# Gated mix of linear and softmax attention on one core: the order of reloads, of the first heads' loads, of the gate and of the linear work

## The chip, the cores and the metric

One core of a Trainium2 chip runs the whole kernel. The metric is the device time of one execution in microseconds (us), the median of several. A core has five engines that run at the same time and meet at semaphores: PE (matrix products), DVE (vector), ACT (scalar functions), POOL (general vector work) and SP (here only a queue that issues DMAs). ACT and POOL issue DMAs as well, each in its own program order.

## The reference

```python
x = A_x                                              # [1, 2048, 1024]
g = _sigmoid((x * gate_w).sum(-1, keepdims=True))    # a gate per row
# A: linear attention, 32 heads of 32, phi(t) = where(t > 0, t + 1, exp(t)) + 1e-6
o_A = (phi(q) @ (phi(k).T @ v)) / (phi(q) @ phi(k).sum(0) + 1e-6)
# B: softmax attention, 32 heads of 32
o_B = softmax(q @ k.T * 32 ** -0.5) @ v
out = g * (o_A @ wo_A) + (1 - g) * (o_B @ wo_B)
```

A and B have their own `wqkv` [1024, 3072] and `wo` [1024, 1024]; all numbers are fp32.

## The kernel before, in words

**Precision.** Each fp32 operand is split into a high and a low part (casts at L304 and L487 on ACT, differences at L299 and L489 on DVE), and a product is three matmuls of 512 columns (`three`, L154, L157, L159). Split operands live in 128x512 places of the large tiles `big0` to `big20`: place 18a is the first half of `big18`, high and low part, 18b the second half.

**Stage A** (to about 563 us) projects x for B and part of A, one half of x's columns at a time (J = 0, then J = 1). For each half there is a pass for v of B with eight weight pieces k = 0 to 7, and then eight "quads" for q and k of B: a quad is seven products (0 to 6) instead of eight. Places for the weights of the quads go round in a ring (`RINGS`): the products 0 to 6 of the last but one quad of the first half use 14a, 19a, 19b, 17b, 14b, 18a, 18b. v's pieces for the second half (`STARTS[1]`) go to 19a, 19b, 17b, 18a, 18b, 14b, 16a, 16b. They were split once and stored in DRAM (`wv0` to `wv7`). `reload_wv` (L822) brings six of them back on ACT's queue (`load_wv_again`, L818), two DMAs each, one piece behind each product from product 1 of that quad on; the last two follow in the last quad.

**Stage B** (from 563 us) is put in order by a planner within the kernel. It keeps a clock for each engine (`T`) and takes steps from four streams: `lin` (linear attention), `max` (row maxima of the scores, matmul L1435 and DVE reduction L1440), `head` (scores again, matmul L1576, then exp on ACT, L1579) and `out` (the projections by `wo`). A head has 64 steps of one `max` and one `head` matmul each; row sums are formed by POOL, whose first sum of a head is L1657 and whose others are L1661; the product with v is L1726. The linear attention's work comes in units of 24 matmuls, in three stages that the text calls kv, q and o (keys, to 1585 us; queries, to 2004 us; output, to 2664 us). After a unit of kv, ACT forms phi (L1315, L1098 to L1100), and DVE (L1321) and POOL (L1326) finish it. How many matmuls of linear attention go with one head step is a number for each stage, `rates`: 2.6 in q (`RATE_Q`), and for kv and o one value that comes out of what is left, (992 + 768 - 24) / (2048 - 320) = 1.005. Nine units of kv are done before the first head step (`WARM_UNITS`), and the maxima start after three of them (`FIRST_UNITS`). Steps that need not be done at once wait in `later` until their planned time (`defer`), or in `tasks`.

**The first heads.** q and k of a head are brought from DRAM (`qk`) to stacks in `big0`/`big1` (head 0) and `big2`/`big3` (head 1): for q 3 pieces for column group 0 and 3 for the rest (`load_q`), for k 3 pieces for each of four column groups (`load_k`), 18 DMAs of together 1.5 MB a head. `load_first` (L1002) issues them on POOL's queue in the steps of `leave`, beside the last quad: the column group 0 of head 0, then that of head 1, each with a step between, then the rest of head 0 and the rest of head 1. Constant rows are set by POOL memsets.

**The gate** is 32 small steps (`gate_step`, L735): SP loads a 128x512 piece of x (`in_xT`), ACT scales it by `gate_w` (L753), POOL adds it up (L759). After every eight, PE sums over the partitions (`total`, L767) and ACT takes the exp (L769). After the last of the four, DVE makes g = 1/(1 + e) and 1 - g (L771 to L773) from it, on 16 columns of SBUF. Gate steps are planned every 2.0 us of planner time from `GATE_FROM` = 4.0 us of stage B on.

Of the kernel before, what the change touches and what calls it, by code (L numbers as in the profile page):

```python
# [12 lines left out]
AF = mybir.ActivationFunctionType  # L13
ALU = mybir.AluOpType
# [6 lines left out]
DH = 32  # L21
# [6 lines left out]

GROUPS, GROUPS_END = (8, 8), (4, 4, 4, 4)
RESERVE = 24.0  # L30
RATE_Q = 2.6
AHEAD = {"head": 0, "max": 6, "lin": 9, "out": 0}
MM = 0.2275
AV, AV_SWITCH = 0.865, 0.35
# [6 lines left out]
NE = 3  # L41
AHEAD_X = 3
PIECE_STEPS, PIECE_REST = (4.0, 3.0), 2
GATE_STEP, GATE_FROM = 2.0, 4.0
LATE = 1.0
MANUAL = {ET.PE, ET.DVE, ET.Activation, ET.SP, ET.Pool}
NMID = 13
# [3 lines left out]
def kernel(  # L51
# [31 lines left out]
    def f32(ap):  # L83
        return ap.bitcast(F32)
# [23 lines left out]
    ones = sb.tile([P, P], F32, name="ones")  # L108
# [5 lines left out]
    g_sb = sb.tile([P, NT], F32, name="g_sb")  # L114
    omg_sb = sb.tile([P, NT], F32, name="omg_sb")
# [12 lines left out]
    bank = [psum.tile([P, C], F32, name=f"bank{i}") for i in range(8)]  # L128
# [34 lines left out]
    def use(eng, cost, *after):  # L163

        T[eng] = max(T[eng], *after, 0.0) + cost
        return T[eng] + LATENCY[eng]

    def dma(to, of):

        T["sp"] = max(T["sp"], T["pe"]) + DMA_ISSUE  # L170
        nc.sync.dma_start(to, of)
# [73 lines left out]
    free = [0.0] * 8  # L245
# [73 lines left out]
    KH = NK // 2  # L319
# [412 lines left out]
    gate_n, gate_at, gate_busy = [0], [GATE_FROM], deque()  # L732
    gate_x, gate_acc = [mid[0], mid[1], mid[8], mid[9], mid[11]], halves(zrep)

    def gate_step():  # L735

        while gate_busy and min(gate_busy)[0] <= T["pe"]:
            first = min(gate_busy)
            gate_busy.remove(first)
            first[-1]()  # L740
        n = gate_n[0]
        if n >= NJ * NK or gate_at[0] > T["pe"]:
            return
        gate_n[0] += 1
        gate_at[0] = T["pe"] + GATE_STEP
        j, k = divmod(n, NK)
        raw, acc = gate_x[n % len(gate_x)], gate_acc[j % 2]
        assert all(at[1] > n - len(gate_x) for at in gate_busy)
        dma(raw, xT[k * P:(k + 1) * P, j * C:(j + 1) * C])

        def times():
            use("act", 0.62, T["pe"])
            nc.scalar.activation(raw if k else acc, raw, AF.Copy, scale=gate_wt[:, k:k + 1])  # L753
            if k:
                plus()

        def plus():
            end = use("pool", 1.3, T["act"] + LATENCY["act"])
            nc.gpsimd.tensor_add(acc, acc, raw)  # L759
            if k == NK - 1:  # L760
                gate_busy.append((end + 0.5, NJ * NK, lambda: tasks.append((bank_at, total))))

        def total():
            b = take()
            end = use("pe", 0.45, free[b])
            for i in range(TPC):
                nc.tensor.matmul(bank[b][:, i:i + 1], acc[:, i * P:(i + 1) * P], ones[:, :1], start=True, stop=True)  # L767
            give(b, use("act", 0.2, end))
            nc.scalar.activation(g_sb[:, j * TPC:(j + 1) * TPC], bank[b][:, :TPC], AF.Exp, scale=-1.0)  # L769
            if j == NJ - 1:  # L770
                nc.vector.tensor_scalar_add(g_sb, g_sb, 1.0)  # L771
                nc.vector.reciprocal(g_sb, g_sb)
                nc.vector.tensor_scalar(omg_sb, g_sb, -1.0, 1.0, op0=ALU.mult, op1=ALU.add)  # L773
                use("dve", 0.4)
                gate_n[0] += 1

        gate_busy.append((T["pe"] + 8.0, n, times))

# [43 lines left out]
    def reload_wv():  # L822

        for _ in range((QUADS - 2) * NP + 1):
            yield
        for k in range(NK - 2):
            load_wv_again(k)
            yield

# [150 lines left out]
    def split_kv(raw, k):  # L980
        split(wpart(k, 0), wpart(k, 1), raw, nc.vector)
# [4 lines left out]
    def leave():  # L986

        split_kv(raw_a[2], 2)
        split_kv(raw_a[3], 3)
        yield  # L990
        split_kv(raw_a[0], 0)
        split_kv(raw_a[1], 1)
        yield
        for k in range(KH, NK):
            split_kv(raw_b[k - KH], k)
            if 0 < k - KH < 3:
                load_first(k - KH - 1, 0)
            yield
        load_first(0, 1)
        load_first(1, 1)  # L1000

    def load_first(h, part):  # L1002

        if not part:
            load_q(h, 0, now=nc.gpsimd)
            load_k(h, 0, nc.gpsimd)
        else:
            load_q(h, 1, NJ, nc.gpsimd)
            for j in range(1, NJ):
                load_k(h, j, nc.gpsimd)  # L1010

    T["sp"] = 0.0

# [366 lines left out]
    tasks = []  # L1380
# [5 lines left out]
    def load_q(h, j, j1=0, now=None):  # L1386

        g, r = divmod(h, 4)
        j1 = max(j + 1, j1)
        q, sl = q_cols(h, j, j1), slice(j * C, j1 * C)  # L1390
        if h < (2 if j else 3):
            nc.gpsimd.memset(f32(q[3 * DH:, :]), 0.0)
        else:
            dma(f32(q[3 * DH:3 * DH + 2, :]), f32(q[3 * DH + 2:3 * DH + 4, :]))
        for b, p in enumerate((0, 0, 1)):
            (now.dma_start if now else dma)(f32(q[b * DH:(b + 1) * DH, :]), qk_d[0][p][g][r * DH:(r + 1) * DH, sl])
        for i in range(j, j1):
            q_ready[h][i] = max(T["pe"] + 8.0, T["sp"] + 5.0)

    def load_k(h, j, now=None):  # L1400

        g, r = divmod(h, 4)
        k = k_stack[h % 2]
        if h < 2 and j == 0:
            nc.gpsimd.memset(f32(k[3 * DH:, :]), 0.0)
            nc.gpsimd.memset(f32(k[3 * DH:3 * DH + 2, :]), 1.0)
        sl = slice(j * C, (j + 1) * C)
        for b, p in enumerate((0, 1, 0)):
            (now.dma_start if now else dma)(f32(k[b * DH:(b + 1) * DH, sl]), qk_d[1][p][g][r * DH:(r + 1) * DH, sl])
        k_ready[h][j] = max(T["pe"] + 6.0, T["sp"] + 4.0)  # L1410

    def v_tile(h):
# [515 lines left out]
    def output():  # L1928
# [55 lines left out]
        for i, (name, n) in enumerate(seq):  # L1984
# [4 lines left out]
            if name == "X21" and n:  # L1989
                load_ra(n + 1)  # L1990

    quad(1, QUADS - 1, beside(leave(), parts))
    assert next(parts, None) is None
    xh_t[2] = sb.tile([P, 2 * HK * P], F32R, name="xh")
    T["sp"] = 0.0
# [2 lines left out]
    for h in range(2):  # L1998
# [121 lines left out]
```

## Time and profile before

| | |
|---|---|
| three runs | 2836.68, 2837.31, 2838.13 us; median 2837.31 us |
| profiled execution | 2837.45 us, of which the span of the trace is 2835.7 us; granted PE clock 0.996 |
| stage kv, 643 to 1585 us | PE busy 933.69 of 942.00 us, POOL 906.13, DVE 796.48, ACT 644.17 |
| stage q, 1585 to 2004 us | PE busy 418.04 of 419.00 us, POOL 373.02 |
| stage o, 2004 to 2664 us | PE busy 659.61 of 660.00 us, POOL 598.99 |

A row of the timeline gives start and length in us, engine, line of the kernel, operation and, in brackets, how long the engine had been idle and on whom it waited. A matmul's recorded length includes the time in the pipeline: at full clock, matmuls of 512 columns stand some 0.23 us apart and read 0.39 us long. A row of the waits gives the waiting line, what it waited for, the total in us, the number of times and the longest. A row of the windows gives the length of the stretch, then busy time and count of PE, its weight loads, DVE, ACT and POOL, the granted clock, the DMA engines' mean busy share and GB/s. A row of the groups gives busy time, mean length in ns and the idle time ahead.

### The profile page before, as it was taken

What the parts mean: (1) busy time and instruction counts of PE and PEld (TensorE: products, weight loads), DVE (VectorE), ACT (ScalarE), POOL (GpSimd) and SP (SyncE); (2) the same over time, 40 slices, a digit from 0 to 9 for tenths busy, and PEclk for the clock granted to TensorE, in tenths of its full rate; (3) what the DMA queues carried; (4) which work ended last, traced back from release to release, by engine and by line L of the source; (5) the groups of instructions that cost most, each with busy time, mean ns of one, the idle gap of its engine ahead of it and who ended that gap; (6) DMA issues with size and microseconds to landing.
All of it is one profiled execution on the core that took longest, in us unless ns stands there. A gap on an engine that the chain in (4) does not pass through costs nothing.

```text
span 2835.7 us, 46700 instructions
## 1 busy us (share of the span) xinstructions
PE 2801.9 (99%) x15784; PEld 2013.6 (71%) x15784; DVE 2267.4 (80%) x3715; ACT 1664.9 (59%) x3167; POOL 2109.6 (74%) x1151
## 2 busy tenths in 40 slices
PE   9998999989999999999999999999999999999999
PEld 8887888876666666676666777676666666676687
DVE  6696759768888888888888877787888888787678
ACT  4333433336676666776666666666767667676622
POOL 0162017468999999999999988998999999999000
PEclk9999999999999999999999999999999999999999
DMA  8587658682443333433334445566544445333774
GB/s 268 174 270 258 202 158 270 222 231 90 103 107 85 86 89 96 114 96 85 85 96 114 142 141 170 172 197 196 168 124 128 128 132 144 101 101 112 261 236 149
DMA packets 391051, 432.77 MB, mean 153 GB/s; under 512 B 105550, under 2 KB 237902, under 8 KB 389020
## 3 DMA queue, kind: packets, MB, share of 16 engines
q1 hardware_dynamic: 366252, 387.69, 45.7%
q0 software_dynamic: 22256, 37.89, 6.2%
q10 hardware_dynamic: 2304, 4.20, 0.4%
q8 instruction: 126, 2.06, 0.3%
q14 instruction: 113, 0.93, 0.1%
HBM read 287.31 MB, written 127.93 MB: 146 GB/s over the span
## 4 chain that ended last, share of the span: by engine, by line
PE 91%; DVE 4%; DMA 3%; ACT 1%; POOL 1%; issue 1%; SPq 0%; ACTq 0%; POOLq 0%; DVEq 0%
PE bank L1726 16%; PE bank L1576 16%; PE bank L1435 15%; PE bank L154 12%; PE bank L157 12%; PE bank L159 12%; PE bank L644 5%; DVE mx L1440 2%; DMA big<-qk 1%; PE bank L1499 1%; ACT big L1579 1%; PE bank L1229 1%; DMA big<-ra 0%; PE bank L1118 0%; DMA big<-big 0%
## 5 line engine op out<-in xcount | busy, mean ns | idle before, releaser
L1661 POOL TENSOR_TENSOR big<-big,big 128x512 f32<-128x512 f32 (+2 forms) x694 | 1641.9, 2370 | 65.4 <-ACT big L1579 19.9
L1440 DVE TENSOR_REDUCE mx<-bank 128x1 f32<-128x512 f32 x2048 | 1285.1, 685 | 282.8 <-PE bank L1435 280.2
L1579 ACT ACTIVATE big<-bank 128x512 f32<-128x512 f32 x2048 | 1156.5, 602 | 349.4 <-PE bank L1576 289.0
L1435 PE MATMUL bank<-big,big 128*128 128x512 f32 x1888 | 743.7, 396 | 13.3 <-DMA big<-qk 7.9
L1576 PE MATMUL bank<-big,big 128*128 128x512 f32 x1888 | 736.2, 396 | 1.0 <-ACT big L1579 0.3
L154 PE MATMUL bank<-big,big 128*128 128x512 f32 x1408 | 552.5, 392 | 10.5 <-DMA big<-wv 8.0
L157 PE MATMUL bank<-big,big 128*128 128x512 f32 x1408 | 551.0, 391 | 0.0
L159 PE MATMUL bank<-big,big 128*128 128x512 f32 x1404 | 549.3, 391 | 1.1 <-DVE big L299 1.1
L1726 PE MATMUL bank<-big,mid 128*32 128x512 f32 x4096 | 454.5, 593 | 0.0
L1576 PEld LDWEIGHTS bank<-big,big 128*128 128x128 f32 x1888 | 353.8, 188 | 125.6 <-issue 45.3
L1435 PEld LDWEIGHTS bank<-big,big 128*128 128x128 f32 x1888 | 355.6, 188 | 101.8 <-DVE mx L1440 12.9
L1726 PEld LDWEIGHTS bank<-big,mid 128*32 128x32 f32 x4096 | 133.4, 110 | 277.4 <-issue 276.0
L154 PEld LDWEIGHTS bank<-big,big 128*128 128x128 f32 x1408 | 265.3, 188 | 71.9 <-DMA big<-wv 8.4
L159 PEld LDWEIGHTS bank<-big,big 128*128 128x128 f32 x1404 | 264.7, 189 | 58.4 <-DVE big L299 2.4
L157 PEld LDWEIGHTS bank<-big,big 128*128 128x128 f32 x1408 | 265.4, 188 | 56.1 <-issue 0.8
L1677 DVE TENSOR_TENSOR bank<-bank,big 128x512 f32<-128x512 f32 x364 | 253.1, 695 | 6.4 <-ACT big L1579 1.4
L304 ACT CAST big<-mid 128x512 fp32r<-128x512 f32 (+1 forms) x169 | 100.2, 618 | 138.6 <-DVE mid L1845 71.7
L299 DVE TENSOR_TENSOR big<-mid,big 128x512 fp32r<-128x512 f32 (+1 forms) x138 | 99.6, 738 | 75.7 <-ACT big L304 75.2
L644 PE MATMUL bank<-big,big 128*128 128x512 f32 x672 | 152.6, 389 | 0.0
L1657 POOL TENSOR_TENSOR big<-big,big 128x1536 f32<-128x1536 f32 (+1 forms) x31 | 132.8, 4285 | 20.4 <-ACT big L1579 20.4
L1734 ACT COPY mid<-bank 128x512 f32<-128x512 f32 x32 | 18.8, 587 | 217.5 <-PE bank L1726 217.5
L644 PEld LDWEIGHTS bank<-big,big 128*128 128x128 f32 x672 | 126.1, 188 | 26.2
(196 smaller groups left out, 2418.9 us busy)
## 6 DMA issues: line engine op xcount, KB each, us to landing
big<-xs SPq DMA_DIRECT2D x202, 256.0 KB
big<-qk SPq DMA_DIRECT2D x690, 64.0 KB
qk<-mid SPq DMA_DIRECT2D x128, 256.0 KB
xh<-xs SPq DMA_DIRECT2D x102, 256.0 KB
big<-oA SPq DMA_DIRECT2D x86, 256.0 KB
xs<-big SPq DMA_DIRECT2D x64, 256.0 KB
oA<-mid SPq DMA_DIRECT2D x64, 256.0 KB
big<-big POOLq DMA_DIRECT2D x50, 256.0 KB, 4.9
```

The costliest lines, as they stand in the source:

```text
L154: yield nc.tensor.matmul(ps, sh, mh_, start=(kt == 0), stop=False)
L157: yield nc.tensor.matmul(ps, sh, ml_, start=False, stop=(late and last))
L159: yield nc.tensor.matmul(ps, sl, mh_, start=False, stop=last)
L644: nc.tensor.matmul(bank[at + i], x_, w_, start=(kt == u == 0 and not onto), stop=(kt == KH - 1 and u == 2), skip_group_check=onto)
L1435: nc.tensor.matmul(bank[b], q[:, t % TPC * P:(t % TPC + 1) * P], k[:, j * C:(j + 1) * C], start=True, stop=True)
L1440: nc.vector.tensor_reduce(m[:, t, j:j + 1], bank[b], AX.X, ALU.max)
L1576: nc.tensor.matmul(bank[b], k[:, t * P:(t + 1) * P], q_cols(h, j), start=True, stop=True)
L1579: nc.scalar.activation(pr_t[i][:, j * C:(j + 1) * C], bank[b], AF.Exp, scale=SCALE)
L1657: nc.gpsimd.tensor_add(lacc[:, :qp], pr(0)[:, :qp], pr(1)[:, :qp])
L1661: nc.gpsimd.tensor_add(lacc[:, sl], lacc[:, sl], pr(t)[:, sl])
L1677: nc.vector.tensor_add(lacc[:, qp:] if t == NT - 1 else l_b[:, :n], l_b[:, :n], src)
L1726: nc.tensor.matmul(av_b[j * DH:(j + 1) * DH, :], v[:, t, :], pr(t)[:, j * C:(j + 1) * C], start=(t == 0), stop=(t == NT - 1))
```

## The change

It has four parts.

1. `reload_wv` takes the pieces in the order 0, 1, 2, 5, 3, 4 instead of 0 to 5.
2. `load_first` brings a whole head at once. Head 0 goes on POOL's queue in the first step of `leave` that splits the second half of the weights; head 1 goes on SP's queue behind the last quad. The memsets follow the DMAs, and those of k are done by column group.
3. `GATE_FROM` is 18.0 instead of 4.0, and the end of each eight gate steps is planned 8.0 instead of 0.5 us after POOL's last add. The last end is done in a bank of PSUM: ACT adds 1, DVE takes the reciprocal there (put off through `defer`), ACT copies g and forms 1 - g.
4. `RATE_KV` = 1.08 is the rate of stage kv; that of o comes out of the rest, (768 - 24) / (2048 - 320 - 992/1.08) = 0.919.

```diff
-RATE_Q = 2.6
+RATE_Q, RATE_KV = 2.6, 1.08
...
-GATE_STEP, GATE_FROM = 2.0, 4.0
+GATE_STEP, GATE_FROM = 2.0, 18.0
...
-                gate_busy.append((end + 0.5, NJ * NK, lambda: tasks.append((bank_at, total))))
+                gate_busy.append((end + 8.0, NJ * NK, lambda: tasks.append((bank_at, total))))
...
-            give(b, use("act", 0.2, end))
             nc.scalar.activation(g_sb[:, j * TPC:(j + 1) * TPC], bank[b][:, :TPC], AF.Exp, scale=-1.0)
-            if j == NJ - 1:
-                nc.vector.tensor_scalar_add(g_sb, g_sb, 1.0)
-                nc.vector.reciprocal(g_sb, g_sb)
-                nc.vector.tensor_scalar(omg_sb, g_sb, -1.0, 1.0, op0=ALU.mult, op1=ALU.add)
-                use("dve", 0.4)
+            end = use("act", 0.2, end)
+            if j < NJ - 1:
+                give(b, end)
+                return
+            pg = bank[b][:, NT:2 * NT]
+            nc.scalar.add(pg, g_sb, ones[:, :1])
+            end = use("act", 0.2, end)
+
+            def invert(end):
+                nc.vector.reciprocal(pg, pg)
+                end = use("act", 0.4, end)
+                nc.scalar.copy(g_sb, pg)
+                nc.scalar.activation(omg_sb, pg, AF.Identity, scale=-1.0, bias=ones[:, :1])
+                free[b] = max(free[b], end)
                 gate_n[0] += 1
+
+            give(b, end, [defer(invert, end, 0.25, 0)])
...
-        for k in range(NK - 2):
+        for k in (0, 1, 2, 5, 3, 4):
             load_wv_again(k)
             yield
...
-            if 0 < k - KH < 3:
-                load_first(k - KH - 1, 0)
+            if k == KH:
+                load_first(0)
             yield
-        load_first(0, 1)
-        load_first(1, 1)
-
-    def load_first(h, part):
-
-        if not part:
-            load_q(h, 0, now=nc.gpsimd)
-            load_k(h, 0, nc.gpsimd)
-        else:
-            load_q(h, 1, NJ, nc.gpsimd)
-            for j in range(1, NJ):
-                load_k(h, j, nc.gpsimd)
+
+    def load_first(h, now=nc.gpsimd):
+        load_q(h, 0, now=now)
+        load_k(h, 0, now)
+        for j in range(1, NJ):
+            load_k(h, j, now)
+        load_q(h, 1, NJ, now)
...
     quad(1, QUADS - 1, beside(leave(), parts))
+    load_first(1, nc.sync)
...
-    rates["kv"] = rates["o"] = (cost["kv"] + cost["o"] - RESERVE) / (steps - cost["q"] / RATE_Q)
+    rates["kv"] = RATE_KV
+    rates["o"] = (cost["o"] - RESERVE) / (steps - cost["q"] / RATE_Q - cost["kv"] / RATE_KV)
```

What this does to the order of the instructions is seen at three places. The lines of the changed file are a few higher (L820 becomes L830, L1315 L1320, L1100 L1105).

The first is ACT's queue in the last but one quad of the first half; `wv3` to `wv5` are the reloaded pieces, `big18` holds places 18a and 18b, `big14` place 14b. Before:

```order
L820 DMA big17_222<-wv2_257 128x512 x2
L304 CAST big17_222<-mid1_225 128x512
L820 DMA big18_1258<-wv3_258 128x512 x2
L487 CAST mid8_232<-mid2_226 128x512
L304 CAST big15_1086<-mid3_227 128x512
L820 DMA big18_1258<-wv4_259 128x512 x2
L487 CAST mid7_231<-mid11_235 128x512
L820 DMA big14_220<-wv5_260 128x512 x2
```

And after the change:

```order
L830 DMA big17_222<-wv2_257 128x512 x2
L304 CAST big17_222<-mid1_225 128x512
L830 DMA big14_220<-wv5_260 128x512 x2
L487 CAST mid8_232<-mid2_226 128x512
L304 CAST big15_1086<-mid3_227 128x512
L830 DMA big18_1258<-wv3_258 128x512 x2
L487 CAST mid7_231<-mid11_235 128x512
L830 DMA big18_1258<-wv4_259 128x512 x2
```

Piece 5 has moved ahead of 3 and 4. The reload of piece 3 used to stand behind product 4 and ahead of product 5, whose weights are in 18a; it stands behind product 5 now, and that of piece 4 behind product 6, which uses 18b.

The second is SP's queue behind the last quad, where `in_xT` is a gate piece, `v0` v of a head, `xs` halves of x for the linear attention's next units, and `qk0`/`qk1` are q and k of a head. Before:

```order
L171 DMA qk1_1_7_159<-mid10_234 128x512
L171 DMA mid0_224<-in_xT 128x512
L171 DMA mid2_226<-v0_160 128x16x32
L171 DMA xh_4530<-xs0_12_75 128x512
L171 DMA xh_4530<-xs1_12_91 128x512
L171 DMA big4_210<-xs0_12_75 128x512
L171 DMA big4_210<-xs1_12_91 128x512
L171 DMA big4_210<-xs0_13_76 128x512
L171 DMA big4_210<-xs1_13_92 128x512
L171 DMA mid1_225<-in_xT 128x512
L171 DMA mid8_232<-in_xT 128x512
```

After the change, with the rows of k's pieces left out:

```order
L171 DMA qk1_1_7_159<-mid10_234 128x512
L1399 DMA big2_208<-qk0_0_0_128 32x512 x2
L1399 DMA big2_208<-qk0_1_0_136 32x512
...
L1399 DMA big2_208<-qk0_0_0_128 32x1536 x2
L1399 DMA big2_208<-qk0_1_0_136 32x1536
L171 DMA mid2_226<-v0_160 128x16x32
L171 DMA xh_4542<-xs0_12_75 128x512
L171 DMA xh_4542<-xs1_12_91 128x512
L171 DMA big4_210<-xs0_12_75 128x512
```

Head 1's 18 DMAs stand ahead of everything else of stage B on this queue, and the first gate piece now follows x's halves instead of leading them.

The third is ACT at the start of stage B: L753 is a gate step, the others are phi of a unit (L1315 to L1100 before, L1320 to L1105 after). Before:

```order
L1315 COPY mid7_231<-bank1_239 128x256
L1098 ACTIVATE mid4_228<-bank1_239 128x256
L1099 ACTIVATE bank1_239<-bank1_239 128x256
L1100 ACTIVATE bank1_239<-bank1_239,eps_193 128x256
L753 ACTIVATE zrep_196<-mid0_224,omg_sb_198 128x512
L753 ACTIVATE mid1_225<-mid1_225,omg_sb_198 128x512
L753 ACTIVATE mid8_232<-mid8_232,omg_sb_198 128x512
L1315 COPY mid7_231<-bank2_240 128x256
```

After the change, from the same unit on:

```order
L1320 COPY mid7_231<-bank1_239 128x256
L1103 ACTIVATE mid4_228<-bank1_239 128x256
L1104 ACTIVATE bank1_239<-bank1_239 128x256
L1105 ACTIVATE bank1_239<-bank1_239,eps_193 128x256
L1320 COPY mid7_231<-bank2_240 128x256
L1103 ACTIVATE mid5_229<-bank2_240 128x256
L1104 ACTIVATE bank2_240<-bank2_240 128x256
L1105 ACTIVATE bank2_240<-bank2_240,eps_193 128x256
L1320 COPY mid7_231<-bank0_238 128x256
L1103 ACTIVATE mid3_227<-bank0_238 128x256
L1104 ACTIVATE bank0_238<-bank0_238 128x256
L1105 ACTIVATE bank0_238<-bank0_238,eps_193 128x256
```

Two more phi now stand ahead of the first gate step. At the end of the gate, the last L753 stands behind the 26th exp of the first head instead of the 8th, ahead of POOL's first sum of that head in both.

More of the change, by code (lines that the diff above doesn't have):

```diff
@@ L1390, in load_q @@
         q, sl = q_cols(h, j, j1), slice(j * C, j1 * C)
-        if h < (2 if j else 3):
-            nc.gpsimd.memset(f32(q[3 * DH:, :]), 0.0)
-        else:
+        if h >= (2 if j else 3):
             dma(f32(q[3 * DH:3 * DH + 2, :]), f32(q[3 * DH + 2:3 * DH + 4, :]))
@@ L1396, in load_q @@
             (now.dma_start if now else dma)(f32(q[b * DH:(b + 1) * DH, :]), qk_d[0][p][g][r * DH:(r + 1) * DH, sl])
+        if h < (2 if j else 3):
+            nc.gpsimd.memset(f32(q[3 * DH:, :]), 0.0)
         for i in range(j, j1):
@@ L1403, in load_k @@
         k = k_stack[h % 2]
-        if h < 2 and j == 0:
-            nc.gpsimd.memset(f32(k[3 * DH:, :]), 0.0)
-            nc.gpsimd.memset(f32(k[3 * DH:3 * DH + 2, :]), 1.0)
         sl = slice(j * C, (j + 1) * C)
@@ L1409, in load_k @@
             (now.dma_start if now else dma)(f32(k[b * DH:(b + 1) * DH, sl]), qk_d[1][p][g][r * DH:(r + 1) * DH, sl])
+        if h < 2:
+            nc.gpsimd.memset(f32(k[3 * DH:, sl]), 0.0)
+            nc.gpsimd.memset(f32(k[3 * DH:3 * DH + 2, sl]), 1.0)
         k_ready[h][j] = max(T["pe"] + 6.0, T["sp"] + 4.0)
```

## The prediction

> **What bounds the kernel now.** I read the page first: is one engine full?
>
> ```profile
> span 2835.7 us, 46700 instructions
> ...
> PE 2801.9 (99%) x15784; PEld 2013.6 (71%) x15784; DVE 2267.4 (80%) x3715; ACT 1664.9 (59%) x3167; POOL 2109.6 (74%) x1151
> ```
>
> PE is busy for 2801.9 of 2835.7 us. Some 34 us are idle, and only they, or matmuls that run slower than they could, can be won without taking work away; the change takes no matmul away. So the next view is what PE waits for (total, times, longest).
>
> ```profile
> PE bank L154 <- DMA big<-wv: 8.0, 1, 8.0
> PE bank L1435 <- DMA big<-qk: 7.9, 2, 7.5
> PE bank L1435 <- DVE mx L1440: 3.4, 1, 3.4
> ```
>
> Three single stops make 19 of the 34 us. The timeline of PE shows each stop, and that it costs more than its idle time. The first, at 254 us, in the last but one "quad" of the first half (rows left out are matmuls alike):
>
> ```profile
> 254.14 0.39 PE L159 MATMUL bank<-big,big 128*128 128x512 f32 x1
> 262.52 0.80 PE L154 MATMUL bank<-big,big 128*128 128x512 f32 x1 [7.99 <-DMA big<-wv]
> ...
> 267.67 0.46 PE L159 MATMUL bank<-big,big 128*128 128x512 f32 x1
> 267.96 0.40 PE L154 MATMUL bank<-big,big 128*128 128x512 f32 x1
> ```
>
> The second, where stage B starts:
>
> ```profile
> 583.26 0.39 PE L157 MATMUL bank<-big,big 128*128 128x512 f32 x1
> ...
> 583.94 0.39 PE L154 MATMUL bank<-big,big 128*128 128x512 f32 x1
> 591.79 0.80 PE L1435 MATMUL bank<-big,big 128*128 128x512 f32 x1 [7.46 <-DMA big<-qk]
> ...
> 595.65 0.39 PE L154 MATMUL bank<-big,big 128*128 128x512 f32 x1
> ```
>
> The third, where the gate ends:
>
> ```profile
> 657.17 0.39 PE L1576 MATMUL bank<-big,big 128*128 128x512 f32 x1
> 660.92 0.79 PE L1435 MATMUL bank<-big,big 128*128 128x512 f32 x1 [3.36 <-DVE mx L1440]
> ...
> 667.34 0.39 PE L154 MATMUL bank<-big,big 128*128 128x512 f32 x1
> ```
>
> From 583.26 to 583.94 are three steps from matmul to matmul, so 0.227 us each. After a stop, the matmuls read 0.6 to 0.8 instead of 0.39 us and stand 0.43 apart until the last row. What a stop costs is therefore the way from the last row ahead of it to the first row at the old pace, less 0.227 for each step in it: 13.82 − 14 × 0.227 = 10.6 us; 11.71 − 10 × 0.227 = 9.4 us; 10.17 − 16 × 0.227 = 6.5 us. Sum 26.6 us. The rest of the idle time lies in gaps of about 1 us and less.
>
> **Part 1: the order of the reloads.** The first stop waits for v's weights, reloaded on ACT's queue. Who ordered that transfer, and when?
>
> ```profile
> 257.77 0.98 ACTq L820 DMA_DIRECT2D big<-wv  x2
> ```
>
> In the order of before, k = 3 is reloaded into place 18a after product 4 of the quad, and product 5 uses 18a: the place is taken again one product too early, so product 5 stands behind a transfer that was issued only at 257.77, 3.6 us after PE had run dry. The same holds for k = 4, place 18b and product 6. After, k = 5 (place 14b, whose product 4 is through) goes there, and 18a and 18b are reloaded behind their own products. No product of the quad then reads a place behind its reload. The two reloads now wait on ACT's queue for products 5 and 6, and the casts for the next quad (L487, L304) stand behind them there, as they already stand behind the first three reloads, which wait for products too. Count of DMAs and their bytes stay. What is late next? The transfers around it:
>
> ```profile
> 245.00:265.00 20.00, 12.01 (x48) 9.20 (x47) 10.93 (x17) 5.67 (x10) 1.80 (x4) 0.81 0.94 301
> 265.00:269.00 4.00, 4.00 (x13) 3.11 (x13) 0.84 (x2) 0.06 (x1) 0.00 (x0) 0.65 0.12 45
> ```
>
> The engines of the DMA are full (0.94, 301 GB/s) up to 265 and nearly empty (0.12) behind it, because the next issues wait for products of the stalled PE. Ten us earlier, PE meets x's halves and v's reloads with 10 us less lead, but the hole of 4 us closes as well. I take the whole 10.6 and keep 5 to 8 us as a possible refund (rival A).
>
> **Part 2: heads 0 and 1, and the later gate.** The page puts the second stop down to a load of q and k. But the load of head 0 is over by then; what ends last is seen by following the bank that L1435 needs: from DVE to ACT to SP.
>
> ```profile
> 591.31 0.42 DVE L1321 SCALAR_TENSOR_TENSOR mid<-mid,bank 128x256 f32<-128x256 f32 x1 [9.32 <-ACT bank L1100]
> ```
> ```profile
> 587.63 0.72 ACT L753 ACTIVATE mid<-mid,omg_sb 128x512 f32<-128x512 f32 x1 [11.24 <-DMA mid<-in_xT]
> ...
> 590.83 0.45 ACT L1100 ACTIVATE bank<-bank,eps 128x256 f32<-128x256 f32 x1
> ```
> ```profile
> 576.36 2.70 SPq L171 DMA_DIRECT2D mid<-in_xT  x3
> ```
>
> ACT's gate step L753 waits 11.24 us for a piece of xT that SP issued at 576.36; phi of the linear attention (L1100) is queued behind it on ACT, DVE's L1321 behind that, the maxima of L1440 behind L1321 on DVE, and PE has no bank. The piece is late since everything moves at once (windows: length, five engines, clock, DMA share, GB/s):
>
> ```profile
> 552.00:565.00 13.00, 13.00 (x59) 10.78 (x58) 8.04 (x14) 3.30 (x6) 12.88 (x17) 1.00 0.52 161
> 565.00:592.00 27.00, 19.47 (x116) 15.53 (x115) 3.92 (x9) 6.75 (x16) 16.93 (x30) 0.94 1.05 246
> ```
>
> 246 GB/s over 27 us are 6.6 MB, with a share of 1.05, while the 13 us ahead ran at 0.52. After, all of head 0 (1.5 MB) is issued one product earlier in the last quad and goes into the half-empty stretch; head 1 leaves POOL for SP, 18 issues ahead of v's tiles, x's halves and the gate's pieces; the first gate step stands on ACT behind the fourth phi instead of the second (GATE_FROM 18 instead of 4). Cost on SP: 18 issues; each of the queue's issues takes about 0.9 us by the row (2.70 for 3), so up to 16 us ahead of x's halves and the gate, of which the queue spends 10 on transfers in any case. Two units of linear attention (24 matmuls each, 5.4 us a unit) and the maxima between them move between ACT's phi and the gate: 11 to 15 us later, against a wait of 11.24. So I expect the stop to go whole (9.4), with a lead of 0 to 5 us, and price the failure at up to 9.4 (rival C). L753 leaves PE without work only if a wait of ACT outlasts the units already issued.
>
> **Part 3: the end of the gate.** The third stop sits on DVE.
>
> ```profile
> 655.18 1.58 DVE L771 TENSOR_SCALAR g_sb<-g_sb 128x16 f32<-128x16 f32 x1
> 656.80 0.25 DVE L772 RECIPROCAL g_sb<-g_sb 128x16 f32<-128x16 f32 x1
> 657.09 3.19 DVE L773 TENSOR_SCALAR omg_sb<-g_sb 128x16 f32<-128x16 f32 x1
> ```
> ```profile
> 653.25 3.48 POOL L1657 TENSOR_TENSOR big<-big,big 128x1536 f32<-128x1536 f32 x1
> 656.81 6.97 POOL L1661 TENSOR_TENSOR big<-big,big 128x1536 f32<-128x1536 f32 x2
> ```
>
> Two operations on 16 columns take 1.58 and 3.19 us and end as POOL's sums end (656.7 and 660.3), while the reciprocal between them takes 0.25. After, DVE keeps one reciprocal on a bank of PSUM; no row shows it there, and its bounds are 0.25 (L772) and 3.5 (one sum of POOL); the nearest row is L772, so 0.3. The add, the copy and 1 − g go to ACT: three operations of about 0.4 us by the phi rows on 256 columns, on an engine that is 59% busy. The reciprocal waits for ACT's add, and the reductions are queued behind it on DVE; it is put off in the program until the add should be through, and a gate's end starts, by the planner's times, 8.0 instead of 0.5 us behind POOL's last add, so I price that wait at nothing, with 3.4 (the stop's idle time) as its bound. The stop goes: 6.5 us.
>
> The skill has a rule that bears on this sum: the Trainium skill, "TensorE: Matmul & The Clock Gate", Part 1, lets the array's clock fall to half only after an idle window of about 3.4 us, on windows that run freely. By it a pause of 3.36 us need not have cost the slow matmuls, and the third stop would be worth about 3.4 instead of 6.5, the sum 23.5. The trace shows the slow pace behind that very pause, so it decides for this execution.
>
> **Part 4: the pace.** Linear attention gets 1.08 matmuls for each head step in stage kv (before 1.005), and 0.919 in stage o (before 1.005). 64 steps, one head, move from kv to o. PE's work is the same. What can be won or lost lies beside it:
>
> ```profile
> 643.00:1585.00 942.00, 933.69 (x5814) 626.70 (x5814) 796.48 (x1372) 644.17 (x1260) 906.13 (x448) 1.00 0.37 97
> ```
> ```profile
> 2085.80:2560.10 474.30, 297.68 (x513) 1.00 0.47 123
> ```
>
> In kv PE idles 8.3 us, of which 3.4 are the third stop: at most 5 us are to be had. In o the exps of ACT (last row: 513 in 474.30 us) give a head of 64 in 59.2 us. After, it has 64 × 0.0856 = 5.5 matmuls less, 1.2 us: 57.9. POOL must keep up with its sums:
>
> ```profile
> 2106.71 4.27 POOL L1657 TENSOR_TENSOR big<-big,big 128x1536 f32<-128x1536 f32 x1
> ...
> 2453.63 4.30 POOL L1657 TENSOR_TENSOR big<-big,big 128x1536 f32<-128x1536 f32 x1
> ```
> ```profile
> 2106.70:2453.60 346.90, 335.53 (x151) 1.00 0.48 126
> ```
>
> Six heads of POOL in 346.92 us are 57.8 us each, without a pause (151 operations, 335.5 us, the rest is 0.08 between two). That is POOL's floor: it was catching up by 1.4 us a head, and after there is 0.1 left. In kv the opposite: a head gets 1.1 us longer, POOL gains room. The late gate takes some of it: its last adds on POOL stand behind the 26th exp instead of the 8th, 18 × 0.93 (59.2/64) = 17 us later, ahead of the first sum. How near POOL was to holding ACT up:
>
> ```profile
> POOL mid L1326 <- ACT big L1579: 6.8, 1, 6.8
> ```
> ```profile
> ACT big L1579 <- POOL big L1661: 1.0, 3, 0.4
> ```
>
> POOL had a pause of 6.8 us in the first head to absorb part of it, and ACT waited for its sums 1.0 us in all of kv. So 0 to 10 us of new waits in the first heads, 0 to 6 in o, against −5 to 0 from the better mix in kv. I take 0 for the sum of these, and −5 to +10 as its bounds.
>
> **The sum.** 2837.45 (profiled execution; 1.7 of it lie around the span, and it is 0.14 over the median of the runs) − 10.6 − 9.4 − 6.5 + 0 = 2810.9; less 0.14: 2811.
>
> **The rivals.**
> A. The first stop comes back: x's halves or the moved reloads meet a DMA already at 0.94. For it: the 301 GB/s; against: the hole of 0.12. Refund 5 to 8: 2816 to 2819.
> B. POOL falls behind, early by the late adds or in o at its floor. For it: the margin of 0.1 us a head, the 1.0 us that ACT waited already; against: 6.8 us of pause. 4 to 12 us: 2815 to 2823.
> C. The second stop only moves: 18 issues on SP ahead of the gate's pieces, and ACT stands at L753 again. 5 to 9.4 us: 2816 to 2820. The edit then doesn't do what it says. If instead the page is right and a qk load was what PE waited for, head 0 loaded whole earlier cures that too.
> D. The other side. In o POOL alone sets the pace: 12.5 heads stand there after the change. It gives back all of 26.6 if POOL's floor is 2.1 us above the 57.9 that PE needs, thus 60.0; each of its 25 operations a head would have to be 0.09 us longer than now. Slower than before by 0.2% needs 2.6 us: 2843. Against: the long sums last alike in both stages.
>
> ```profile
> L1661 POOL TENSOR_TENSOR big<-big,big 128x1536 f32<-128x1536 f32 x151 | 529.5, 3507 | 9.7
> ```
> ```profile
> L1661 POOL TENSOR_TENSOR big<-big,big 128x1536 f32<-128x1536 f32 x104 | 364.0, 3500 | 11.7 <-ACT big L1579 3.8
> ```
>
> **How the numbers follow.** Forecast (all three stops gone, rest within −5 to +4) 0.55, 2806 to 2815; A 0.11; B 0.16; C 0.12; D 0.02; two of A to C together 0.04, to about 2832. The range takes the forecast and A, B and C up to 2823; below, it goes to the bound of −5 and another 3, since each stop's cost is uncertain by about 1: 2803 to 2823. A measurement of this kernel can tell about 0.2% from no change, 5.7 us. Faster by more than that: all but D and a part of the pairs, 0.94; within it 0.04; slower 0.02.
>
> **What would show it.** Right: no wait of PE over 3 us left; no L154 waiting for wv near 254; L753's first step with a short wait and no pause of PE near 584; one reciprocal of about 0.3 us at the gate's end. In o, L1657 stands 57.8 to 58.0 us apart. Wrong: a wait of L1579 for POOL's sums of several us (B), of L753 for in_xT (C), of a matmul for xs or wv between 255 and 300 (A), or L1657 more than 59 apart in o (D).

## The result, and the profile after

The changed kernel takes 2821.71 us in the median of four runs (2819.13 to 2822.47), the kernel before 2837.47 (2836.68 to 2838.13): ratio 0.9941, 95% interval [0.9928, 0.9953]. That is 15.8 us less, 59% of the 26.6 that were forecast, inside the range, but above the forecast proper (2806 to 2815) and at the place where rival B had put it (2815 to 2823). The spans of the two profiled executions differ by nearly the same amount, 15.3 us (2835.7 to 2820.4), so they can be compared row by row. First the page of the changed kernel and its PE waits (total, times, longest); lines are those of the changed file, some 5 higher:

```profile
span 2820.4 us, 46781 instructions
...
PE 2796.0 (99%) x15784; PEld 2010.3 (71%) x15784; DVE 2268.8 (80%) x3713; ACT 1662.6 (59%) x3170; POOL 2102.9 (75%) x1145
```
```profile
PE bank L1496 <- POOL big L1666: 5.4, 1, 5.4
PE bank L1581 <- ACT big L1584: 2.9, 1, 2.9
PE bank L1440 <- ACT big L1584: 2.2, 2, 1.4
PE bank L1504 <- DMA big<-big: 1.8, 2, 1.1
```

None of the three old waits is in the list. The four rows that lead it now are new; their stops lie at 2610, at 1140, at 667 and 1147, and around 772 us. Where the first stop was, the timeline of PE goes on at the old pace, and the DMA hole of 4 us (0.12, 45 GB/s) is filled:

```profile
254.19 0.39 PE L159 MATMUL bank<-big,big 128*128 128x512 f32 x1
254.41 0.39 PE L154 MATMUL bank<-big,big 128*128 128x512 f32 x1
```
```profile
245.00:265.00 20.00, 20.00 (x90) 16.57 (x89) 15.05 (x23) 6.92 (x12) 2.05 (x4) 1.00 0.94 304
265.00:269.00 4.00, 4.00 (x19) 3.30 (x19) 0.00 (x0) 1.16 (x2) 0.00 (x0) 1.00 1.06 399
```

At the start of stage B, PE is busy for 26.93 of 27 us (before 19.47), and ACT's first gate step no longer waits at all:

```profile
565.00:592.00 27.00, 26.93 (x163) 21.78 (x162) 22.41 (x41) 8.97 (x21) 8.73 (x8) 1.00 0.82 218
```
```profile
580.65 0.71 ACT L753 ACTIVATE zrep<-mid,omg_sb 128x512 f32<-128x512 f32 x1
```

Its piece of x, issued at 571.2, was there when the fourth phi, which stands ahead of it, was through. The first exp comes 20.1 us earlier than before (643.60 to 623.50), which is what the first two stops were to give (20.0). From there on, nothing more was won: the end is 15.3 us earlier. Four of the signs named in advance came: no wait for wv near 254, L753 without a wait, the short reciprocal, and POOL's first sums 57.8 us apart in o (2502.73 and 2560.55, the last two). The fifth did not: a wait of PE over 3 us is left, at 2610. The first sum of POOL shows why the heads did not gain:

```profile
623.50 1.28 ACT L1584 ACTIVATE big<-bank 128x512 f32<-128x512 f32 x2 [1.21 <-PE bank L1581]
```
```profile
645.57 1.30 POOL L759 TENSOR_TENSOR zrep<-zrep,mid 128x512 f32<-128x512 f32 x1 [1.62 <-ACT mid L753]
...
647.53 3.48 POOL L1662 TENSOR_TENSOR big<-big,big 128x1536 f32<-128x1536 f32 x1
```

It starts 24.0 us behind the first exp, behind the gate's last add; before, it was 9.6 (653.25 and 643.60). And at the end, where PE wants the sums of the last heads:

```profile
2609.73 0.39 PE L157 MATMUL bank<-big,big 128*128 128x512 f32 x1
2615.56 1.94 PE L1496 MATMUL bank<-big,ones 128*32 128x512 f32 x8 [5.44 <-POOL big L1666]
```

The gate's end has its one short reciprocal, 0.27 us. DVE waits 6.93 us for ACT in front of it. That cost PE nothing, as it was priced, because PE was at 60 products with v meanwhile (649.62 to 656.24 us):

```profile
657.77 0.27 DVE L778 RECIPROCAL bank<-bank 128x16 f32<-128x16 f32 x1 [6.93 <-ACT bank L774]
```

### The profile page after: what moved, and what is told of

It reads as the page before. It is cut to its first block, busy times and chain, and to the rows that moved or that the text cites. A ratio compares the mean times of both kernels' runs of the same rounds, so it can differ in the third digit from the quotient of the medians.

```text
span 2820.4 us, 46781 instructions
## 1 busy us (share of the span) xinstructions
PE 2796.0 (99%) x15784; PEld 2010.3 (71%) x15784; DVE 2268.8 (80%) x3713; ACT 1662.6 (59%) x3170; POOL 2102.9 (75%) x1145
## 4 chain that ended last, share of the span: by engine, by line
PE 90%; DVE 4%; POOL 3%; DMA 2%; ACT 1%; issue 1%; SPq 0%; DVEq 0%; POOLq 0%; ACTq 0%
PE bank L1731 15%; PE bank L1581 15%; PE bank L1440 15%; PE bank L154 12%; PE bank L157 12%; PE bank L159 12%; PE bank L644 5%; POOL big L1666 3%; DVE mx L1445 2%; DMA big<-ra 1%; PE bank L1504 1%; PE bank L1234 1%; DVE big L1903 1%; DMA big<-big 1%; ACT big L1584 1%
## 5 line engine op out<-in xcount | busy, mean ns | idle before, releaser
L1445 DVE TENSOR_REDUCE mx<-bank 128x1 f32<-128x512 f32 x2048 | 1283.1, 682 | 280.6 <-PE bank L1440 278.3
```

Of the source, the lines that this page charges most:

```text
L1445: nc.vector.tensor_reduce(m[:, t, j:j + 1], bank[b], AX.X, ALU.max)
```

## The experiments

Two questions were left: what each part of the change gives alone, and who took back the 11 us. Theory G puts it down to the late gate, which sets POOL behind; theory F to the new rates, since POOL is at its floor in o. The executions of one kernel lie 1.5 to 10 us apart, so a difference of 2 us in the medians says little; the rows of the traces carry the readings.

**Each part alone, added to the kernel before.** The order of the reloads:

```diff
-        for k in range(NK - 2):
+        for k in (0, 1, 2, 5, 3, 4):
```

> The kernel before with the new order of v's reloads alone. Theory S (the stops are independent and add up): the stop at 254 us goes whole, 10.3 to 10.6 us, so about 2827.0 us, and the stops at 584 and 657 stand 10 us earlier and keep their size. Rival R (DMA is full there, something else is late next): a wait for xs or wv appears between 255 and 300, or the stop of stage B grows, and 5 us or less are left: 2832 us or more.

2825.38 us, ratio 0.9958 [0.9943, 0.9973]; span 11.7 us shorter. The first exp comes at 633.2 instead of 643.6, 10.4 us earlier, and the next stop stands where it was, only earlier:

```profile
573.07 0.39 PE L154 MATMUL bank<-big,big 128*128 128x512 f32 x1
581.11 0.80 PE L1435 MATMUL bank<-big,big 128*128 128x512 f32 x1 [7.65 <-DVE mid L1321]
```

No wait for xs or wv appears behind 255. Theory S holds for this part; rival A of the prediction falls. The row also names another releaser for the same stop: DVE's L1321, the link of the chain that the prediction followed, instead of a qk load. The other 1.3 us of the span are won at the third stop. It is as long as before (3.38 us of idle time), but the half pace behind it ends sooner:

```profile
650.52 0.80 PE L1435 MATMUL bank<-big,big 128*128 128x512 f32 x1 [3.38 <-DVE mx L1440]
...
653.65 0.40 PE L1576 MATMUL bank<-big,big 128*128 128x512 f32 x1
```

Counted as in the prediction, from the matmul at 646.75, it costs 6.90 − 8 × 0.227 = 5.1 us instead of 6.5.

The gate's end in PSUM. The edit is the part of the change from `total` on; the planned time of the end stayed at 0.5 us in this run, though the expectation says 8.0; the run after it has both.

> The kernel before with the end of the gate on ACT and in PSUM and with the later start of that end (8.0 instead of 0.5 us of planner time), the gate steps where they were. Theory S: the stop at 657 us goes, 6.5 us, so about 2831 us, and no other wait of PE grows. Rival P (POOL's sums are what holds the first heads, and DVE's two slow operations only hid it): POOL's pace gives it back in the next 200 us, 2835 us or more.

2835.32 us, ratio 0.9994 [0.9985, 1.0003]; span 1.5 us shorter. The stop at 657 is gone. But windows show what came 25 us behind it:

```profile
680.00:690.00 10.00, 9.49 (x36) 6.25 (x34) 9.97 (x18) 6.87 (x14) 9.76 (x4) 1.00 0.28 95
690.00:700.00 10.00, 9.65 (x37) 7.43 (x37) 7.24 (x13) 7.20 (x15) 9.77 (x7) 0.83 0.08 24
```

DVE works 9.97 of 10 us, PE follows its reductions, and in the next 10 us the granted clock is 0.83. Counted like a stop, from 686.35 to the row at 694.53 (both are shown in the last section), this costs 8.18 − 17 × 0.227 = 4.3 us of the 6.5 that the stop had cost, which leaves 2.2; the medians differ by 2.0. Neither theory foresaw this; rival P's number is met, but not by POOL, which waits and works as before. A full DVE alone does not do it: the kernel before (first row) and the changed kernel (second row) have one as well, and PE keeps its full pace there, 43 and 44 matmuls in 10 us.

```profile
690.00:700.00 10.00, 9.90 (x43) 7.55 (x42) 9.96 (x19) 7.99 (x18) 9.84 (x4) 1.00 0.31 92
690.00:700.00 10.00, 10.00 (x44) 7.86 (x44) 10.00 (x18) 9.26 (x20) 9.69 (x9) 1.00 0.39 92
```

What the slow stretch has and these have not is seven matmuls for the maxima (L1445) in a row, at the 0.6 us of DVE's reductions, with no other matmul between them. Seven in a row stand in the kernel before as well, at 876 and 1000 us, but they are through in 2.8 us instead of 4, and the clock stays at 1.00.

With the planned time as in the change:

```diff
-                gate_busy.append((end + 0.5, NJ * NK, lambda: tasks.append((bank_at, total))))
+                gate_busy.append((end + 8.0, NJ * NK, lambda: tasks.append((bank_at, total))))
```

> The kernel before with both edits at the gate's end: in PSUM and on ACT, and planned 8.0 instead of 0.5 us behind POOL's last add (the run with the first edit alone had kept 0.5). There the stop at 657 us was gone, but a stretch at 684 to 696 us in which DVE has no pause, and PE falls to half pace behind a wait of 0.6 us, took 3 of the 6.5 us back. Theory D (DVE's reductions hold PE in these heads, and the stop only hid it): it stays, 2833 to 2837 us. Rival W (that stretch is an accident of the planned order, which the 8.0 us change): it goes, 2829 to 2832 us.

2836.29 us, ratio 0.9996 [0.9987, 1.0004]; the same stretch is there at 685 to 690. Theory D's time is met. PE's order differs from that of before in both kernels, from 655 us on in the first and from 601 us on in this one, since the planner goes on from other clocks. So the order of the maxima, and not DVE's load alone, may be what counts; that was not shown. The gate's end was not taken back out of the changed kernel, so what it is worth there was not measured.

The late gate:

```diff
-GATE_STEP, GATE_FROM = 2.0, 4.0
+GATE_STEP, GATE_FROM = 2.0, 18.0
```

> The kernel before with the gate steps from 18.0 us of stage B on and nothing else. Theory G (the later place cures the stop at 584 us, and POOL pays for it): the first head step comes about 9.5 us earlier, POOL's first sum stands more than 20 us behind the first exp instead of 9.6, and the heads up to the tenth give back 8 to 15 us: 2832 to 2840 us. Rival L2 (the late gate is a plain gain, the losses come only with the new rates): 2826 to 2829 us.

2833.85 us, ratio 0.9988 [0.9979, 0.9998]; span 3.4 us shorter. The stop at 584 is gone and the first exp comes 11.5 us earlier (1.5 of them from a shorter first stop). POOL's first sum then stands 24.2 us behind it:

```profile
632.07 1.28 ACT L1579 ACTIVATE big<-bank 128x512 f32<-128x512 f32 x2 [0.73 <-PE bank L1576]
```
```profile
656.29 3.47 POOL L1657 TENSOR_TENSOR big<-big,big 128x1536 f32<-128x1536 f32 x1
```

Of the 11.5 us, 8.1 are given back by the end. Theory G holds, at the old rates; L2 falls.

**Parts taken back from the changed kernel.** The early gate:

```diff
-GATE_STEP, GATE_FROM = 2.0, 18.0
+GATE_STEP, GATE_FROM = 2.0, 4.0
```

> The changed kernel with the gate steps from 4.0 us of stage B on, as before. Theory G (the late gate puts POOL behind by about 10 us, and from there come the waits of PE at 666, 772 and 1139 to 1148 us, together about 8 us): those go; the first gate step meets the full DMA again, so that 0 to 9 us come back near 575 us: 2814 to 2822 us. Theory F: the waits in kv stay within 2 us of what they are, the stop at 2610 stays too, and with the stop near 575 the time is 2822 to 2830 us.

2816.47 us (2815.43 to 2818.11), ratio 0.9928 [0.9913, 0.9943]: 5.2 us below the changed kernel. Its waits of PE:

```profile
PE bank L1440 <- DVE mid L1326: 7.3, 1, 7.3
PE bank L1496 <- POOL big L1666: 5.5, 1, 5.5
PE bank L1440 <- ACT big L1584: 1.8, 1, 1.8
```

The stop at the start of stage B is back in full, as ACT's second gate step waits for its piece again although the loads of heads 0 and 1 are the new ones. POOL's first sum is 10.2 us behind the first exp, and PE's waits in kv are down from 7.9 to 2.0 us (600 to 1150 us).

```profile
577.85 1.40 ACT L753 ACTIVATE mid<-mid,omg_sb 128x512 f32<-128x512 f32 x2 [7.67 <-DMA mid<-in_xT]
```
```profile
633.23 0.60 ACT L1584 ACTIVATE big<-bank 128x512 f32<-128x512 f32 x1 [2.56 <-PE bank L1581]
```
```profile
643.45 3.51 POOL L1662 TENSOR_TENSOR big<-big,big 128x1536 f32<-128x1536 f32 x1
```

The first exp is 9.7 us later than in the changed kernel (633.23 to 623.50), the end 5.2 us earlier: the late gate won 9.7 us at its start and lost 14.9 behind it. Theory G again. The stop at 2610 stays, and POOL's lag in the last of its heads is 19.9 us in both kernels, so that stop isn't the gate's.

How a late POOL reaches PE in kv is seen at the changed kernel's wait of 2.9 us at 1140. It is not that exps wait for POOL's sums (3.5 us in all, 0.8 at most). SP's next loads of weights need places that POOL's L1054 must leave first, and one of these issues waits 12.2 us for it; ACT's cast stands behind that load, and the exps that free PE's banks behind the cast:

```profile
1125.62 13.95 SPq L171 DMA_DIRECT2D big<-in_a_wqkv  x4
```
```profile
1141.44 0.62 ACT L1052 CAST big<-big 128x512 fp32r<-128x512 f32 x1 [3.54 <-DMA big<-in_a_wqkv]
```

With the early gate the same issue waits 7.9 us, and PE 1.8 us. These waits explain 6 of the 14.9 us; the granted clock, 0.97 in two stretches (735 to 803 and 1134 to 1202 us) where it is 1.00 with the early gate, explains some more, and the rest was not traced to single waits.

The old loads of heads 0 and 1:

```diff
-            if k == KH:
-                load_first(0)
+            if 0 < k - KH < 3:
+                load_first(k - KH - 1, 0)
...
-    load_first(1, nc.sync)
```

> The changed kernel with the loads of heads 0 and 1 on POOL's queue in the old order. Theory L (it is the later place of the gate steps on ACT alone that cures the stop at 584 us; with the new loads but the early gate it was still there): no wait of PE over 3 us between 560 and 600, 2819 to 2823 us as the changed kernel. Rival M (the loads' new order is needed too, since SP's gate pieces and x's halves land too late beside POOL's loads): a stop of 4 us or more stays there, 2826 to 2831 us.

2822.11 us, ratio 0.9947 [0.9933, 0.9962]; no wait over 3 us between 560 and 600. Theory L holds: the stop at 584 is cured by the gate's place on ACT, and the new loads give nothing that can be measured (0.4 us in the medians).

The old rates:

```diff
-RATE_Q, RATE_KV = 2.6, 1.08
+RATE_Q, RATE_KV = 2.6, 1.0046296296296295
```

> The changed kernel with the old rate, 1.0046 in kv and in o. Theory F (POOL is at its floor of 57.8 us a head in o, so the new rate of o costs the stop of 5.8 us at 2610 us): that stop goes, L1657's counterpart lags less behind its head towards the end, and the time falls by 4 to 6 us to about 2816. Rival G (the late gate alone put POOL behind, the rate has no part in it): the stop at 2610 stays, and in kv, where a head gets 1.1 us shorter, the waits at 1139 to 1148 grow: 2822 to 2826 us.

2823.43 us (2822.15 to 2825.59), ratio 0.9954 [0.9938, 0.9971]. The waits:

```profile
PE bank L1504 <- DMA big<-big: 4.7, 3, 2.6
PE bank L1440 <- DMA big<-qk: 2.2, 3, 1.4
PE bank L1440 <- ACT big L1584: 2.1, 5, 1.0
```

Half of each theory: the stop at 2610 is gone (F; POOL's first sum of the last head that it adds up is 11.4 us behind that head's first exp, instead of 19.9), and in kv, where POOL has less room, PE's waits are more (G; 11.5 us between 600 and 1585 us, 8.2 in the changed kernel). The time is the same within what can be told.

A rate between:

```diff
-RATE_Q, RATE_KV = 2.6, 1.08
+RATE_Q, RATE_KV = 2.6, 1.04
```

> The changed kernel with a rate of 1.04 in kv, and so 0.961 in o. Theory F (the stop at 2610 us comes from POOL's floor of 57.8 us a head in o): a head of o gets 0.6 us longer, POOL's lag falls to 12 to 14 us by the last head, the stop goes or falls under 1 us; kv's small waits stay: 2816 to 2819 us. Rival H (what the rate gives in kv by a better mix of matmuls is worth as much as the stop): the stop goes but the time stays at 2820 to 2824 us, as with the old rate.

2818.70 us (2818.41 to 2824.98), ratio 0.9943 [0.9926, 0.9959].

```profile
PE bank L1440 <- ACT big L1584: 3.0, 4, 2.0
PE bank L1581 <- ACT big L1584: 2.3, 1, 2.3
PE bank L1440 <- DMA big<-qk: 1.9, 1, 1.9
```

The stop at 2610 is gone, with a last lag of 11.5 us, as F says. Two waits are new, for a load of q and k at the switch from q to o (1949 us) and for another load in o (2129 us). The median is in F's range, but one of four runs at 2825 leaves H open. The same rate was tried with the early gate (both edits as above):

> The changed kernel with a rate of 1.04 in kv and the gate from 4.0 us on, as before. If POOL's floor in o (F) and the late gate (G) are the two that took the gain, the stop near 575 us is here (about 9 us), the one at 2610 is not, and the waits of the first heads are not: 2810 to 2814 us. If what the rate saves at the end is lost again in kv (H): 2815 to 2819 us, as with the gate from 4.0 alone.

2820.17 us (2818.61 to 2824.13), ratio 0.9941 [0.9929, 0.9953], 3.7 us more than with the early gate alone. The stop at 2610 is gone here too. Of the three waits that lead, the first is the stop at the start of stage B (581 us), as always with the early gate; the other two are those at 1949 and 2131 us:

```profile
PE bank L1440 <- DVE mid L1326: 7.7, 1, 7.7
PE bank L1440 <- DMA big<-qk: 2.6, 1, 2.6
...
PE bank L1581 <- DMA extra<-ml: 1.6, 1, 1.6
```

So H holds for the time, though not only in the way it was put: what the rate saves at 2610 is lost at these two waits and in small amounts in kv. And theory G's price is not one number. At this rate the late gate comes out ahead: its first exp is 9.0 us earlier (632.45 to 623.45), its end 2.8 us (spans 2819.1 and 2816.3), so it gives back 6.2 us, where it gave back 8.1 at the old rates and 14.9 at 1.08.

**Versions that should have been better.** The gate from 10.0, with the change's rate and with 1.04:

```diff
-GATE_STEP, GATE_FROM = 2.0, 18.0
+GATE_STEP, GATE_FROM = 2.0, 10.0
```

> The changed kernel with the gate steps from 10.0 instead of 18.0 us of stage B on: the first stands on ACT behind the third unit's phi, and the last behind the 16th exp instead of the 26th. Theory G (each exp by which the gate ends earlier brings POOL 0.9 us nearer, so 9 us in all; the waits of PE in the first heads and at 1140 to 1150 us go, and the first piece of x for the gate, which lands near 578 us, holds phi by 1 us at most): 2811 to 2816 us. Rival (the stop near 575 returns as soon as one gate step stands ahead of the fourth phi): a wait of 3 us or more there and 2816 to 2822 us.

> The changed kernel with both, 1.04 in kv and the gate from 10.0 us on. If theories F and G hold and add up: no stop at 2610 us, the waits of the first heads gone, 2807 to 2812 us. If the better mix of kv is worth the stop (rival H): the same as with the gate from 10.0 us alone, 2811 to 2816 us.

2817.08 us (2814.30 to 2821.66; ratio 0.9931 [0.9916, 0.9946]) and 2817.22 us (2811.26 to 2821.14; ratio 0.9928 [0.9913, 0.9943]). POOL's first lag is 14.7 us in both. The stop near 575 does not return, but the gate's pieces now stand ahead of a half of x on SP's queue, and PE waits 2.9 and 2.4 us for it at 592. The first is in the rival's range, its wait just under the 3 us that were named; the second lies above both ranges that were given for it. The profiled execution of the second, 2811.26, is the fastest of the study; the others of that kernel are 5 to 10 us slower. Their granted clocks are 0.998 to 0.999, while this one has 1.000, no spell of half pace at all; over 2810 us, 0.002 of the clock is 5.6 us by estimate. Half pace thus makes about half of the spread or more; the rest was not settled.

Last, the gate begun late and ended early:

```diff
-GATE_STEP, GATE_FROM = 2.0, 18.0
+GATE_STEP, GATE_FROM = 1.6, 12.0
```

> The changed kernel with the gate steps from 12.0 us on and every 1.6 instead of 2.0 us: the first stands on ACT behind the third unit's phi, the last behind the 8th exp, as in the kernel before. Theory G (what counts for POOL is where the gate ends, for the stop at 584 us where it begins): both are had, no stop over 3.5 us between 570 and 600, POOL's first sum 12 us or less behind the first exp, 2807 to 2813 us. Rival (the faster loads of x meet a full DMA, so x's halves or the gate's pieces come late): one or more waits of 3 us and more between 575 and 620, 2814 to 2820 us.

2818.61 us (2816.68 to 2820.53), ratio 0.9934 [0.9921, 0.9948]. POOL's first lag is 9.3 us as meant, but the rival was right:

```profile
PE bank L154 <- DMA xh<-xs: 5.6, 2, 4.3
PE bank L1496 <- POOL big L1666: 5.4, 1, 5.4
PE bank L1440 <- ACT big L1584: 3.2, 1, 3.2
```

Halves of x for the linear attention came late at 592 and 628 us. All these versions lie between 2816 and 2819 us and can't be told apart; the early gate (2816.47) has the lowest median.

## Why the prediction was right, and where it was too high

Sign and range were right; the gain was forecast too high by 10.8 us. The range held because it took in rival B, to which the prediction gave 16 in 100; the forecast itself, with its 55, was missed. By its own steps:

- **Part 1, 10.6 us.** Right in cause and size: alone it moves the first exp by 10.4 us. (The rows from 254.14 to 267.96 are 13 steps and not 14, so the sum should read 10.9.) The 5 to 8 us kept as a refund were not needed; the DMA took the load in the hole of 4 us.
- **Part 2, 9.4 us.** Right that the gate step on ACT, not the qk load that the page of the profile names, ends the wait: the stop returns when the gate goes back to its early place and the new loads stay, and it stays away when the loads go back and the gate stays late. 9.7 us, measured at the first exp. Moving head 0 and head 1 played no measured part, where the prediction had let both edits share the credit.
- **Part 3, 6.5 us.** The stop went and its cause is as described (the reciprocal takes 0.27 us). Alone it was worth only 1.5 to 2 us: a stop's whole way was taken as gained without asking what comes next, and 25 us later seven maxima in a row hold PE and bring the half pace back. In the changed kernel that stretch is not there (the granted clock is 1.00 from 640 to 740 us), so this does not explain the 10.8 us.
- **Part 4, 0 us.** This is the term that was mis-sized. Its two dangers both came. POOL stood 14 us later in the first head (24.0 against 10.2; worked out as 17), with 6 us more waits of PE in kv, and the late gate lost 14.9 us over the whole run against the early one. And there was the stop of 5.4 us at 2610, because POOL, at 57.8 us a head in o, could not make up its lag (19.9 us at the end, before 11.3). I had both mechanisms and gave them 16 in 100 and a zero in the sum. A price with the bounds 0 and +10 in the first heads and 0 to 6 in o, against a gain of at most 5, has no zero in its middle. The better mix in kv did not pay for them: with the old rates the time is the same.
- **Sum.** By spans, the parts alone give −11.7 (reloads), −3.4 (late gate) and −1.5 (gate's end), and the changed kernel without its loads is 1.5 longer, without its rates the same: −18.1 against −15.3 measured, within what single executions differ by. That is no proof that the parts add up: the late gate is worth −3.4 alone, but +5.2 in the changed kernel and −2.8 with a rate of 1.04.

Where the 10.8 us went can be counted from the starts of PE's matmuls. Taking as lost what each matmul of 512 columns on the whole array stands over 0.227 us from the next, the changed kernel loses 24.1 us less than the kernel before up to 760 us, so nearly all that the three stops were to give was had. Behind that it loses 5.6 us more at 2600 to 2640 and 1.0 more from 760 to 1200, and some 3 us less elsewhere; the products of other shapes, with the waits behind them, take 6.8 us longer (with the early gate 1.7). What holds the other products was not followed.

## What to carry to other kernels

A step that is moved off one engine's way stands later in the next engine's queue: price it there with its delay, the more so where that engine is nearly full (POOL here works 904 of 942 us in kv). A stop's length is what its removal is worth only if PE finds work in the order behind it; look at the 50 us behind the stop, and put a one-sided risk into the sum, not only into the range. And where the profile names a releaser that was done long before, follow the chain through the engines: here that found the edit that mattered.

## What the runs showed of the hardware

How long PE may stop before matmuls fall to half pace is not one number, nor how long the half pace lasts: the same third stop (3.36 and 3.38 us) was followed by it to 667 us, 6 us long, in the kernel before and for only 3 us with the new reloads alone. In the changed kernel with the old loads, two stops follow each other within 10 us:

```profile
1136.47 0.39 PE L1445 MATMUL bank<-big,big 128*128 128x512 f32 x1
1140.03 0.50 PE L1586 MATMUL bank<-big,big 128*128 128x512 f32 x1 [3.16 <-ACT big L1589]
1140.52 0.50 PE L1445 MATMUL bank<-big,big 128*128 128x512 f32 x1
...
1142.95 0.39 PE L1586 MATMUL bank<-big,big 128*128 128x512 f32 x1
1146.63 0.80 PE L1445 MATMUL bank<-big,big 128*128 128x512 f32 x1 [3.30 <-ACT big L1589]
1147.23 0.63 PE L1586 MATMUL bank<-big,big 128*128 128x512 f32 x1
```

After 3.16 us of idle time PE goes on nearly at full pace (0.50, soon 0.39), after 3.30 us at half (0.80, then 0.63). The Trainium skill, "TensorE: Matmul & The Clock Gate", Part 1, puts the fall behind an idle window of about 3.4 us, of windows that run freely. The rows agree only roughly: the idle times of the three short stops here that half pace followed, 3.30, 3.36 and 3.38 us, are a little under a whole window, and in the changed kernel the pace is half from 1144.02 us on, 1.4 us behind a stop of only 2.88. That the place of the stop in the window decides was not shown.

Nor does it take a stop of this length. This is PE with the gate's end in PSUM:

```profile
686.35 1.33 PE L1445 MATMUL bank<-big,big 128*128 128x512 f32 x3
687.84 2.24 PE L1445 MATMUL bank<-big,extra 128*128 128x512 f32 x4 [0.15 <-ACT big L1589]
690.42 0.69 PE L1586 MATMUL bank<-big,big 128*128 128x512 f32 x1 [0.35 <-DVE mx L1450]
690.92 0.63 PE L157 MATMUL bank<-big,big 128*128 128x512 f32 x1
...
694.53 0.39 PE L157 MATMUL bank<-big,big 128*128 128x512 f32 x1
```

For 4 us seven matmuls follow DVE's reductions, most of them 0.6 us apart. The idle times are 0.15 and 0.35 us only, because a recorded length includes the time in the pipeline, and the pace is half behind them, to about 694 us. The same page of the Trainium skill tells of a kernel whose short, frequent pauses have the same effect ("A second HAM failure mode: psum-queue depth-cycling"); the rows here agree, with one such fall.
